# Six batches of Linformer attention inside a gated feed-forward kernel: from three mixed groups of TensorE work per batch to six single ones, with two Q buffers and the second batch's loads ahead of the loop

## The chip, the cores and the metric

One core of a Trainium2 chip. The metric is the device time of one execution in microseconds, lower being better. Engines are called PE (TensorE; PEld are its weight loads), DVE (VectorE), ACT (ScalarE), POOL (GpSimd) and SP (SyncE). POOL and SP issue the DMAs here.

## The reference

Eight batches (B = 8), eight heads, 1024 rows, head width 64. K and V are first projected along the rows to 64 by E and F, so that the scores of a head are 1024 x 64. A gated feed-forward layer follows.

```
k_proj = einsum('ks,bhsd->bhkd', E, k)
v_proj = einsum('ks,bhsd->bhkd', F, v)
scores = q @ k_proj^T / 8 ;  attn = softmax(scores)
x      = attn @ v_proj, heads side by side        # (8192, 512)
out    = (sigmoid(x @ w_gate) * (x @ w_val)) @ w_out   # 512 -> 1536 -> 512
```

Inputs and output are float32; the kernel's matmuls take bfloat16.

## The kernel before, in words

**A planner and five queues.** The program is a list of operations written in the order of the source. `add` (line 38) notes which tiles and PSUM banks an operation reads and writes; `emit` then gives each engine its own operations in that order, with a semaphore wait for each dependence on another engine. So the source order is the order of every queue, and nothing is reordered later. `mm`, `act`, `dve`, `pool` and `load` (lines 213 to 239) are the helpers that add to PE, ACT, DVE, POOL and POOL's DMA queue; all matmuls have line 221, all ACT instructions line 225, all loads line 239.

**PSUM.** Eight banks of 128 x 512 float32. Rings hand them out in turn: `ffn` has four (pF), `att` four (pA); the first batch uses `whole`, an order over both that is written out by hand.

**Feed-forward part.** A batch is two blocks of 512 rows. `mstep(blk, m)` (line 953) is one of 12 steps of a block: four matmuls for the gate (G), four for the value (V), each into an `ffn` bank; then `gate` (line 985): tanh on ACT from the G bank into `sig`, and on DVE `(sig + 1) * V` into `hT`. `oproj(blk, tt)` (line 1005) is an output projection: 12 matmuls, a scaling on DVE into `ost`, a DMA from SP. There are four per block, and they run during the next block.

**Slots.** For each batch b the loop at line 1095 makes a list `todo` of these pieces; the pieces are called slots here. For b >= 1 there are 32: with m for a step and o for a projection, slots 0 to 15 are m0 m1 m2 o0 m3 m4 m5 o1 m6 m7 m8 o2 m9 m10 m11 o3, and slots 16 to 31 the same for the second block. `put(i, fn)` hangs attention work of batch b+1 behind slot i. The iteration of batch b thus does the attention of batch b+1.

**Attention of a batch.** Its pieces: `kv`, 16 matmuls that project K and V into the halves of one bank; `keep_kd`, an ACT copy to `kpd` and a transposing DMA from SP into `kpD`; `keep_vd`, two ACT copies to `vpD`; `sc_one`, four score matmuls of 64 x 64 tiles for one pair of heads, and `exp_one`, two exponentials on ACT into `eT`; `den`, eight matmuls that sum `eT`; `rec(c)`, a reciprocal on DVE for a quarter of the columns; `gather`, four SP DMAs that bring the reciprocals into rows; `spread`, eight POOL broadcasts into `rb`; `xo_one`, four output matmuls for one pair of heads; `mul`, two DVE multiplications of the outputs with `rb` into `xT`, the input of the feed-forward part.

For batches 2 to 7 (iterations 1 to 6) the pieces stand in three groups on PE. `scores`: the scores of three of the four pairs, 12 matmuls, using two `ffn` and four `att` banks. `mixed`: the scores of the last pair and the outputs of two pairs, 12 matmuls. `outputs`: the outputs of the other two pairs, K and V of the batch after, and the sums, 32 matmuls. Outputs go from PSUM to SBUF on ACT (`keep_x`, into `xu`), and the multiplications read `xu`. The reciprocals hang on four slots, 12 to 15 or 17 to 20. In iteration 1 `kv2` at slot 3 projects K and V of batch 2.

Batch 0 and batch 1 are apart. Batch 0 runs in two halves (`half_unit`), the first before the loop, the second at slots 4 to 9 of iteration 0. Batch 1 (iteration 0) runs as single pieces: `k_alone`, `turn_k`, `sc(0)`, `sc(1)`, `den`, the reciprocals, `v_alone`, `split`, `bc`, `xo(0)`, `xo(1)`; there the multiplications read PSUM.

**Loads.** POOL's queue starts with batch 0 and the weights. `second_loads` (line 1076) follows slot 5 of iteration 0: Q, K and V of batch 1, Q's transposes on SP (`transpose_q`, four DMAs into `qT`), `wO`, a library for POOL. There is one Q buffer `Qb` and one `qT`; K and V turn through three `KV` buffers. `load_next` issues K, V and Q of a later batch.

Of the kernel before, what the change touches and what calls it, by code (L numbers as in the profile page):

```python
# [6 lines left out]
AF = mybir.ActivationFunctionType  # L7
ALU = mybir.AluOpType
# [4 lines left out]
P = 128  # L13
# [105 lines left out]
def bass_linformer_attn__then__ffn_glu_sigmoid_kernel(  # L119
# [18 lines left out]
    with contextlib.ExitStack() as es:  # L138
# [21 lines left out]
        Qb = sbuf("Qb", [P, H, S // P * DH], BF16)  # L160
# [5 lines left out]
        qT = sbuf("qT", [P, H, 512], BF16)  # L166
# [6 lines left out]
        xu = sbuf("xu", [P, 8, 512], FP32)  # L173
# [67 lines left out]
        def turned():  # L241
            return [("qT", r) for r in range(NR)]

        def load_k(b):
            n = 2 * b % 3
            load(
                KV[n][:, :, :],
                k[b].rearrange("h (p t) d -> p h (t d)", t=NT),
                [("KV", n, 0), ("KV", n, 1)],
                f"KV{n}",  # L250
                r=turned() if b >= 2 else (),
            )
# [19 lines left out]
        def load_q(b):  # L272
            load(
                Qb[:, :, :],
                q[b].rearrange("h (p t) d -> p h (t d)", t=NT),
                [("Q", hf, R) for hf in range(2) for R in range(2)],
                "Q",
            )

        def load_q_half(b, hf, R):  # L280
            cc, hh = slice(256 * hf, 256 * hf + 256), slice(4 * R, 4 * R + 4)
            load(
                Qb[:, hh, cc],
                q[b].rearrange("h (p t) d -> p h (t d)", t=NT)[:, hh, cc],
                [("Q", hf, R)],
                f"Q{hf}{R}",
            )
# [235 lines left out]
        def half_unit(hf, ring):  # L523

            s = 0
            qv = qT[:, :, :].rearrange("p (R x) c -> p R x c", R=2)

            def qt(R, engines):
                for rr, eng in enumerate(engines):
                    bk = ring.next()  # L530
                    ob = bank[bk][:, :].bitcast(BF16)
                    for x in range(2):
                        for t in range(2):
# [4 lines left out]
                                Qb[:, 4 * R + 2 * rr + x, (2 * hf + t) * P : (2 * hf + t + 1) * P],  # L538
                                ident[:, :],
                                [("Q", hf, R), "ident"],  # L540
# [4 lines left out]
                    ws = [("qT", hf, R, rr)]  # L545
# [5 lines left out]
            def sc(R):  # L551
                bks = [ring.next(), ring.next()]
                for rr in range(2):
                    for c in range(2):
                        h = 4 * R + 2 * rr + c
                        for g in range(2):
# [5 lines left out]
                                qT[gg, h, 256 * hf : 256 * hf + 256],  # L562
                                [("kpD", R), ("qT", hf, R, rr)],
# [94 lines left out]
        def transpose_q():  # L658
            for r in range(NR):
                add(  # L660
                    "SP",
                    lambda e, r=r: e.dma_start_transpose(
                        qT[:, 2 * r : 2 * r + 2, :].rearrange("p h (t c) -> p (h t) c", c=P),
                        Qb[:, 2 * r : 2 * r + 2, :].rearrange("p h c -> p (h c)"),
                    ),
                    r=[("Q", hf, r // 2) for hf in range(2)],
                    w=[("qT", r)] + [("qT", hf, r // 2, r % 2) for hf in range(2)],
                    dma=f"qT{r}",
                )

        def kv(b, bk):
            for t in range(NT):
                for w in range(2):
                    n = (2 * b + w) % 3
                    src = KV[n][:, :, :].rearrange("p h (t d) -> p t h d", t=NT)
                    mm(
                        bk,
                        bank[bk][64 * w : 64 * w + 64, :],
                        EFT[:, t, 64 * w : 64 * w + 64],
                        src[:, t, :, :],  # L680
                        [("KV", n, 0), ("KV", n, 1), ("EFT", t // 4)],
                        start=(t == 0),
                        stop=(t == NT - 1),
                        tp=(0, 64 * w),
                    )

        def keep_kd(bk):
            act(
                kpd[:, :, :, :],
                bank[bk][0:64, :]  # L690
                .rearrange("p (h d) -> p h d", h=H)
                .unsqueeze(2)
                .to_broadcast([64, H, 2, DH]),
                [],
                ["kpd"],
                b=bk,
            )
            add(
                "SP",
                lambda e: e.dma_start_transpose(  # L700
                    kpD[:, :, :],
                    kpd[:, :, :, :].rearrange("p h g d -> p (h g d)"),
                ),
                r=["kpd"],
                w=[("kpD", 0), ("kpD", 1)],
                dma="kpD",
            )

        def keep_vd(bk):
            for g in range(2):  # L710
                act(
                    vpD[64 * g : 64 * g + 64, :, :].rearrange("p h d -> p (h d)"),
                    bank[bk][64:128, :],
                    [],
                    [("vpD", h, g, R) for h in range(2) for R in range(2)],
                    b=bk,
                )

        def attention(b):
            s = b % 2  # L720
            den_bank = []

# [10 lines left out]
            def sc_one(r, bks):  # L733
                for c in range(2):
                    h = 2 * r + c
                    for g in range(2):
                        gg, oo = slice(64 * g, 64 * g + 64), 64 * (g ^ c)
                        mm(
                            bks[g],
                            bank[bks[g]][oo : oo + 64, :],  # L740
                            kpD[gg, h, :],
                            qT[gg, h, :],
                            [("kpD", r // 2), ("qT", r)],
                            tp=(64 * g, oo),
                        )

            def exp_one(r, bks):
                for g in range(2):
                    act(
                        eT[:, 2 * r + g, :],  # L750
                        bank[bks[g]][:, :],
                        [],
                        [("eT", 2 * r + g)],
                        b=bks[g],
                        func=AF.Exp,
                        scale=SCALE,
                    )

            def sc(r2):
                for r in (2 * r2, 2 * r2 + 1):  # L760
                    bks = [att.next(), att.next()]
                    sc_one(r, bks)
                    exp_one(r, bks)

            def den():
# [14 lines left out]
                den_bank.append(bk)  # L780

            def rec(c):
                cc, bk = slice(c * P, (c + 1) * P), den_bank[0]
# [54 lines left out]
            def xo_one(r, bks):  # L838
                for g in range(2):
                    n = 2 * r + g  # L840
                    for c in range(2):
                        kk = slice(64 * (g ^ c), 64 * (g ^ c) + 64)
                        mm(
                            bks[g],
                            bank[bks[g]][64 * c : 64 * c + 64, :],
                            vpD[kk, 2 * r + c, :],
                            eT[kk, n, :],
                            VPD(r // 2) + [("eT", n)],
                            tp=(64 * (g ^ c), 64 * c),
                        )  # L850

            def keep_x(r, bks):
                for g in range(2):
                    n = 2 * r + g
                    act(xu[:, n, :], bank[bks[g]][:, :], [], [("xu", n)], b=bks[g])

            def mul(r, bks=None):
                for g in range(2):
                    n = 2 * r + g
                    x = xu[:, n, :] if bks is None else bank[bks[g]][:, :]  # L860
                    dve(
                        lambda e, r=r, g=g, n=n, x=x: e.tensor_tensor(  # L862
                            xT[s][:, r, :, 256 * g : 256 * g + 256],
                            x.rearrange("p (f c) -> p f c", f=2),
                            rb[:, n, :].rearrange("p (f c) -> p f c", f=2),
                            ALU.mult,
                        ),
                        [("rb", n)] + ([("xu", n)] if bks is None else []),
                        [("xT", s, r, 0, g), ("xT", s, r, 1, g)],
                        b=None if bks is None else bks[g],  # L870
                    )

            def xo(r2):
                for r in (2 * r2, 2 * r2 + 1):
                    bks = [att.next(), att.next()]
                    xo_one(r, bks)
                    mul(r, bks)

            if b == 1:
# [5 lines left out]
                    lambda: (den(), rec(0)),  # L885
                    lambda: rec(1),
                    lambda: rec(2),
                    v_alone,
                    lambda: rec(3),
# [6 lines left out]

            held = {}

            def two(ring):
                return [ring.next(), ring.next()]  # L900

            def scores():
                f, a0, a1 = two(ffn), two(att), two(att)
                for r, bks in ((2, f), (0, a0), (1, a1)):
                    sc_one(r, bks)
                exp_one(2, f)
                exp_one(0, a0)
                held["sc"] = a1

# [284 lines left out]
```

## Time and profile before

| | |
|---|---|
| median of 3 runs (564.53 to 564.6) | 564.6 us |
| the profiled execution | 564.6 us |
| its span, first to last instruction | 562.8 us |
| granted TensorE clock | 1.000 |
| matmuls of the feed-forward part (wG, wV; wO) | 768 and 768; 780, of 3032 in all |
| mean of a 128 x 512 matmul, overlapping the next | 379 ns |
| tanh of a gate on ACT, x192 | 602 ns |
| gate's multiplication on DVE, x192 | 685 ns |
| multiplication xT<-xu,rb, x48; xT<-pA,rb, x8 | 856 ns; 680 ns |
| reciprocal of a quarter, x28 | 951 ns |

Busy shares are over the whole span. Matmuls overlap, so PE's price of a piece is read from starts, not from durations: the distance from the start of one matmul to the start of the next is its pitch. In the views below, "pF<-xT,wG" is a matmul into an `ffn` bank from `xT` and `wG`, "x4" the number merged in one line, and the two first columns are start and length in microseconds.

### The profile page before, as it was taken

The page shows a single profiled execution, that of the slowest core. Times are in us where ns is not written, and L with a number is a line of the kernel's source. Part 1 is how long each engine was busy: PE and PEld are TensorE (multiplying, and loading weights), DVE is VectorE, ACT ScalarE, POOL GpSimd, SP SyncE. Part 2 cuts the span into 40 slices and gives each one's busy share as a digit, 9 for nine tenths or more (in the row PEclk, how much of TensorE's full clock was granted, in tenths as well). Part 3 has the DMA queues.
Part 4 walks back from the last instruction along what each step waited for, and adds up shares of the span by engine and source line. Part 5 has one row for each costly group of instructions (what it writes and reads, how often), then busy time and mean ns, then how long its engine had stood idle before and what let it go on. Part 6 is the DMA issues. An engine that isn't in the chain of part 4 may idle for free.

```text
span 562.8 us, 7706 instructions
## 1 busy us (share of the span) xinstructions
PE 551.9 (98%) x3032; PEld 248.8 (44%) x3032; DVE 258.5 (46%) x397; ACT 200.8 (36%) x362; POOL 113.0 (20%) x148
## 2 busy tenths in 40 slices
PE   5899999999999999999999999999999999999998
PEld 4444434444444444444444444444444444444444
DVE  4544463325733564335643447335553357433332
ACT  2654633444244422534226422354224432222220
POOL 9210200102800190003600064000800026000000
PEclk9999999999999999999999999999999999999999
DMA  9999999953493259314591057901511101110012
GB/s 163 199 194 189 143 218 191 171 116 63 95 210 76 48 102 201 73 38 87 107 210 40 20 123 113 187 20 47 97 37 39 37 23 39 37 38 24 33 37 94
DMA packets 76564, 56.01 MB, mean 100 GB/s; under 512 B 34704, under 2 KB 68240, under 8 KB 76528
## 3 DMA queue, kind: packets, MB, share of 16 engines
q0 software_dynamic: 33984, 29.89, 34.6%
q1 hardware_dynamic: 42544, 25.63, 17.7%
q8 instruction: 24, 0.39, 0.3%
q14 instruction: 12, 0.10, 0.1%
HBM read 60.29 MB, written 16.78 MB: 137 GB/s over the span
## 4 chain that ended last, share of the span: by engine, by line
PE 96%; DMA 2%; DVE 1%; POOL 0%; issue 0%; ACT 0%; POOLq 0%
PE pF L221 90%; PE pA L221 6%; DMA Qb<-in_q_dram 2%; DVE xT L645 1%; POOL KV L239 0%; DVE hT L992 0%; DVE rden L593 0%; ACT qT L225 0%; POOL quad L313 0%; DVE rhl L596 0%; DVE ost L1023 0%; DVE rhi L594 0%; POOLq L1179 0%
## 5 line engine op out<-in xcount | busy, mean ns | idle before, releaser
L225 ACT ACTIVATE sig<-pF 128x512 f32<-128x512 f32 x192 | 115.5, 602 | 296.3 <-PE pF L221 290.6
L992 DVE SCALAR_TENSOR_TENSOR hT<-sig,pF 128x512 bf16<-128x512 f32 x192 | 131.4, 685 | 167.5 <-PE pF L221 129.0
L221 PE MATMUL pF<-xT,wG 128*128 128x512 bf16 x768 | 198.0, 379 | 1.2 <-DVE xT L645 1.2
L221 PE MATMUL pF<-xT,wV 128*128 128x512 bf16 x768 | 197.8, 379 | 0.3 <-DVE hT L992 0.3
L221 PE MATMUL pF<-wO,hT 128*128 128x512 bf16 (+1 forms) x780 | 175.7, 376 | 0.0
L831 POOL PARTITION_BROADCAST rb<-rrow x96 | 77.0, 862 | 286.3 <-DMA rrow<-rden 281.1
L221 PEld LDWEIGHTS pF<-wO,hT 128*128 128x128 bf16 x780 | 75.2, 98 | 91.4 <-issue 3.3
L221 PEld LDWEIGHTS pF<-xT,wV 128*128 128x128 bf16 x768 | 75.0, 98 | 91.1 <-DVE hT L992 0.8
L221 PEld LDWEIGHTS pF<-xT,wG 128*128 128x128 bf16 x768 | 72.9, 98 | 94.1 <-issue 8.7
L1023 DVE TENSOR_SCALAR ost<-pF 128x512 f32<-128x512 f32 (+1 forms) x65 | 44.4, 683 | 110.4 <-PE pF L221 110.4
L862 DVE TENSOR_TENSOR xT<-xu,rb 128x512 bf16<-128x512 f32 x48 | 39.2, 856 | 0.0
L785 DVE RECIPROCAL rden<-pA 128x128 f32<-128x128 f32 x28 | 26.6, 951 | 12.3 <-PE pA L221 12.3
L225 ACT ACTIVATE eT<-pA 128x512 bf16<-128x512 f32 x39 | 21.3, 626 | 1.6 <-PE pA L221 1.6
L225 ACT ACTIVATE eT<-pF 128x512 bf16<-128x512 f32 x25 | 13.6, 595 | 22.6 <-PE pF L221 22.4
L225 ACT ACTIVATE xu<-pA 128x512 f32<-128x512 f32 x36 | 19.1, 617 | 0.0
L221 PE MATMUL pA<-KV,EFT 128*64 128x512 bf16 (+2 forms) x168 | 16.0, 332 | 0.3
L239 POOL DMA_DIRECT2D KV<-in_k_dram x9 | 8.0, 885 | 34.5 <-PE pF L221 34.4
L239 POOL DMA_DIRECT2D Qb<-in_q_dram x11 | 9.4, 866 | 16.5 <-PE pF L221 16.5
L221 PEld LDWEIGHTS pA<-KV,EFT 128*64 128x64 bf16 x168 | 8.3, 115 | 7.8 <-issue 3.3
L225 ACT ACTIVATE vpD<-pA 64x512 bf16<-64x512 f32 (+2 forms) x22 | 10.2, 466 | 2.4 <-PE pA L221 1.9
L221 PE MATMUL pA<-eT,vpD 64*64 64x512 bf16 (+1 forms) x116 | 8.8, 355 | 0.0
L225 ACT ACTIVATE rb<-pA 128x512 f32<-128x512 f32 x14 | 7.4, 601 | 2.1 <-PE pA L221 2.1
(72 smaller groups left out, 122.3 us busy)
## 6 DMA issues: line engine op xcount, KB each, us to landing
out_dram<-ost SPq DMA_DIRECT2D x63, 256.0 KB, 2.0
Qb<-in_q_dram POOLq DMA_DIRECT2D x7, 1024.0 KB, 19.8
KV<-in_k_dram POOLq DMA_DIRECT2D x7, 1024.0 KB, 9.9
KV<-in_v_dram POOLq DMA_DIRECT2D x7, 1024.0 KB, 14.9
wO<-in_moe_w_out_dram POOLq DMA_DIRECT2D x1, 1536.0 KB, 12.2
wG<-in_moe_w_gate_dram POOLq DMA_DIRECT2D x5, 256.0 KB, 18.7
wV<-in_moe_w_val_dram POOLq DMA_DIRECT2D x5, 256.0 KB, 19.1
KV<-in_k_dram POOLq DMA_DIRECT2D x2, 512.0 KB, 8.9
```

What stands on the lines that cost most here:

```text
L221: return add("PE", lambda e: e.matmul(o, lhsT, rhs, **kw), r=r, x=[("bank", b)])
L225: return add("ACT", lambda e: e.activation(o, i, func, scale=scale), r=r, w=w, x=x)
L239: add("POOL", lambda e: e.dma_start(o, i), r=r, w=w, dma=sem)
L645: lambda e, g=g, o=o: e.tensor_tensor(o, bank[bks[g]][:, :].rearrange("p (r c) -> p r c", r=2), rb[:, 2 * R + g, :].rearrange("p (r c) -> ...
L785: lambda e: e.reciprocal(rden[:, cc], bank[bk][:, cc]),
L831: lambda e, n=n, i=2 * rnd + c, j=j, parts=parts: e.partition_broadcast(rb[0:parts, n, :], rrow[32 * j : 32 * j + 1, i, :], channels=parts),
L862: lambda e, r=r, g=g, n=n, x=x: e.tensor_tensor(xT[s][:, r, :, 256 * g : 256 * g + 256], x.rearrange("p (f c) -> p f c", f=2), rb[:, n, :] ...
L992: lambda e: e.scalar_tensor_tensor(hT[blk % 2][:, m, :], sg[:, :], 1.0, bank[pv][:, :], ALU.add, ALU.mult,),
L1023: lambda e, pb=pb, c0=c0, c1=c1: e.tensor_scalar(o[:, c0:c1], bank[pb][:, 0 : c1 - c0], 0.5, None, op0=ALU.mult),
```

## The change

Batches 2 to 7 no longer run in three mixed groups but as six single pieces per batch, all of the batch itself: `kv` at slot 3 (with its ACT copies), `turn_kd` at 6, `sc(0)` at 10, `sc(1)` at 13, `den` with its four reciprocals and then `gather` at 16, `spread` at 20 and 23, `xo(0)` at 26, `xo(1)` at 29. Each score or output piece is two pairs of heads, 8 matmuls. They use the `att` banks alone. `xu` and its copies go; the multiplications read PSUM. `Qb` and `qT` get a second buffer, picked by the batch's parity, and all names of their tiles get that index. `load_next` has the order K, Q, V. What was `second_loads` stands ahead of the loop. Batches 0 and 1 keep their pieces and slots.

```diff
-        Qb = sbuf("Qb", [P, H, S // P * DH], BF16)
+        Qb = [sbuf(f"Qb{i}", [P, H, S // P * DH], BF16) for i in range(2)]
-        qT = sbuf("qT", [P, H, 512], BF16)
+        qT = [sbuf(f"qT{i}", [P, H, 512], BF16) for i in range(2)]
-        xu = sbuf("xu", [P, 8, 512], FP32)
...
         def load_k(b):
-                r=turned() if b >= 2 else (),
+                r=turned(b - 1) if b >= 2 else (),
...
+            def turn_kd():
+                add("SP", lambda e: e.dma_start_transpose(kpD[:, :, :], ...),
+                    r=["kpd"], w=[("kpD", 0), ("kpD", 1)], dma="kpD")
...
             def den():
...
-                den_bank.append(bk)
+                if b == 1:
+                    den_bank.append(bk)
+                else:
+                    for c in range(4):
+                        rec(c, bk)
...
             def xo(r2):
                 for r in (2 * r2, 2 * r2 + 1):
                     bks = [att.next(), att.next()]
-                    xo_one(r, bks)
-                    mul(r, bks)
+                    for g in range(2):
...
+                            mm(bks[g], ..., VPD(r // 2) + [("eT", n)], tp=(64 * (g ^ c), 64 * c))
...
+                        dve(lambda e, r=r, g=g, n=n, bk=bks[g]: e.tensor_tensor(
+                                xT[s][:, r, :, 256 * g : 256 * g + 256],
+                                bank[bk][:, :].rearrange("p (f c) -> p f c", f=2),
+                                rb[:, n, :].rearrange("p (f c) -> p f c", f=2),
+                                ALU.mult), ...)
...
             return [
-                scores,
-                lambda: exp_one(1, held["sc"]),
-                mixed,
-                lambda: keep_x(1, held["x"]),
-                outputs,
-                lambda: (keep_x(3, held["x"]), rec(1)),
-                lambda: (rec(2), keep_kd(held["kv"]) if b + 1 < B else None),
-                lambda: (rec(3), gather(), keep_vd(held["kv"]) if b + 1 < B else None),
-                lambda: (spread(0), spread(1)),
-                lambda: mul(0),
-                lambda: mul(1),
-                lambda: mul(2),
-                lambda: mul(3),
+                kv,
+                turn_kd,
+                lambda: sc(0),
+                lambda: sc(1),
+                den,
+                gather,
+                lambda: spread(0),
+                lambda: spread(1),
+                lambda: xo(0),
+                lambda: xo(1),
             ]
...
-        def second_loads():
-            load_q(1)
-            load_k(1)
-            load_v(1)
-            transpose_q()
-            load(wO[:, :, :], ..., r=turned())
-            ...
+        load_q(1)
+        load_k(1)
+        load_v(1)
+        transpose_q(1)
+        load(wO[:, :, :], ..., r=turned(1))
...
-                put(5, second_loads)
...
-            elif b == 1:
-                put(3, kv2)
-                spots = (8, 9, 11, 12, 17, 18, 19, 20, 20, 25, 27, 28, 30)
             else:
-                spots = (3, 4, 6, 7, 12, 13, 14, 15, 15, 21, 23, 25, 27)
+                spots = (3, 6, 10, 13, 16, 16, 20, 23, 26, 29)
...
             def load_next(n):
                 load_k(n)
+                load_q(n)
                 load_v(n)
-                load_q(n)
...
-                put(24, transpose_q)
-            elif b + 2 < B:
-                put(4 if b == 1 else 1, lambda b=b: load_next(b + 2))
-                put(20 if b == 1 else 16, transpose_q)
+                put(24, lambda: transpose_q(2))
+            else:
+                if b + 2 < B:
+                    put(4, lambda b=b: load_next(b + 2))
+                    put(20, lambda b=b: transpose_q(b + 2))
```

## The prediction

> **What bounds the kernel now.** I read the page first, then who waited for whom on PE, then PE's own order of time around the attention groups, then single instructions on the other engines and the landings of the loads. The page's first part and its chain of waits:
>
> ```profile
> PE 551.9 (98%) x3032; PEld 248.8 (44%) x3032; DVE 258.5 (46%) x397; ACT 200.8 (36%) x362; POOL 113.0 (20%) x148
> ...
> PE 96%; DMA 2%; DVE 1%; POOL 0%; issue 0%; ACT 0%; POOLq 0%
> ```
>
> PE is 96% of the chain. The waits view, PE's lines:
>
> ```profile
> PE pA L221 <- DMA EF<-in_F_dram: 5.4, 1, 5.4
> PE pF L221 <- DVE xT L645: 1.2, 3, 0.8
> PE pA L221 <- DMA Qb<-in_q_dram: 0.5, 1, 0.5
> PE pF L221 <- DVE rhl L596: 0.4, 1, 0.4
> PE pF L221 <- DVE hT L992: 0.3, 1, 0.3
> ```
>
> All of these lie before 49 us (E, F and the first batch). From there to the end PE waits for nothing, so the later part costs what PE needs to push its instructions through. The stage view, cut at one batch of steady state (columns: stretch and length, then busy time and instructions of PE, weight loads, DVE, ACT and POOL, then granted clock, DMA share, GB/s):
>
> ```profile
> 229.69:296.65 66.96, 66.96 (x350) 29.55 (x344) 31.25 (x45) 24.36 (x43) 15.26 (x19) 1.00 0.50 97
> ```
>
> The next three batches take 66.96 us each too, all at a granted clock of 1.00. 288 of the matmuls are the feed-forward part's. PE's order of time gives their pitch: eight start between 163.09 and 164.82, 0.216 us each, so 62.2 us; the other 4.8 us are attention. **The question is only what attention costs PE in the new grouping.** The price of a group is the start of the feed-forward matmul after it, less the start of the run before it, less 0.216 for each matmul of that run. The old groups (scores; scores with outputs; outputs with K/V and sums):
>
> ```profile
> 161.57 0.81 PE L221 MATMUL pF<-wO,hT 128*128 128x512 bf16 x3
> 162.31 0.41 PE L221 MATMUL pF<-qT,kpD 64*64 64x512 bf16 x4
> 162.55 0.60 PE L221 MATMUL pA<-qT,kpD 64*64 64x512 bf16 x8
> 163.09 1.04 PE L221 MATMUL pF<-xT,wG 128*128 128x512 bf16 x4
> ...
> 180.38 1.03 PE L221 MATMUL pF<-xT,wV 128*128 128x512 bf16 x4
> 181.34 0.41 PE L221 MATMUL pF<-eT,vpD 64*64 64x512 bf16 x4
> 181.57 0.39 PE L221 MATMUL pA<-eT,vpD 64*64 64x512 bf16 x4
> 181.89 1.92 PE L221 MATMUL pA<-KV,EFT 128*64 128x512 bf16 x16
> 183.74 0.61 PE L221 MATMUL pA<-eT,dsel 128*32 128x512 bf16 x8
> 184.29 1.04 PE L221 MATMUL pF<-xT,wG 128*128 128x512 bf16 x4
> ```
>
> 163.09 - 161.57 - 3 x 0.216 = 0.87 us for twelve; the mixed group at 168.37 also has twelve and also costs 0.87; 184.29 - 180.38 - 4 x 0.216 = 3.05 us for the third. One batch: 0.87 + 0.87 + 3.05 = 4.79. The second batch still runs the old small groups, which are the ones that the change brings back:
>
> ```profile
> 56.88 1.03 PE L221 MATMUL pF<-xT,wV 128*128 128x512 bf16 x4
> 57.84 0.63 PE L221 MATMUL pA<-qT,kpD 64*64 64x512 bf16 x8
> 58.39 1.04 PE L221 MATMUL pF<-xT,wG 128*128 128x512 bf16 x4
> ```
>
> 58.39 - 56.88 - 0.864 = 0.65 for eight score matmuls (0.67 for the next eight). By the same subtraction the eight matmuls of the sums at 62.63 cost 0.70, the eight outputs at 79.11 and at 82.37 cost 0.65 each, and the sixteen of K and V alone at 93.39 cost 1.94. Twelve cost 0.87 and eight 0.65, so four packed ones take one pitch, 0.216, and some 0.22 of each group is going in and coming out.
>
> **Part by part.**
>
> *Regrouping.* Six batches, iterations 1 to 6. Before: iteration 1 has K/V alone and the three groups, 1.94 + 4.79 = 6.73; iterations 2 to 5 have 4.79 each; iteration 6 has no K/V, 0.87 + 0.87 + 1.20 = 2.94 (its last group at 449.22 costs 1.20). Sum 28.8. After: 1.94 + 0.65 + 0.67 + 0.70 + 0.65 + 0.65 = 5.26, times six = 31.6. **+2.8 us.** Same matmuls; what is added is three more goings in and out per batch, less the two changes of kind inside the third group, which cost 3.05 - (0.43 + 1.73 + 0.43) - 0.22 = 0.24 together.
>
> *Copies into xu gone.* 48 ACT copies (25.6 us busy) go, and the 48 multiplications read PSUM: 0.68 us as in the second batch in place of a mean 0.856. Neither stands on the chain: worth 0. Its counterpart is that a multiplication now holds the bank of its output. xo(0) and xo(1) come three slots apart, some 6 us, and four multiplications took 2.47, so the banks are free.
>
> *Four reciprocals in a row, after slot 16.* Counted from the end of slot 16: the gate of slot 16 runs at 0.27 to 0.9, the sums end on PE at 0.7, the reciprocals run from 1.0 to 4.9 (0.95 each). Queued behind them on DVE is the gate of slot 17, ready at 2.7, now 4.9 to 5.5, then that of slot 18, to 6.2. PE needs the V bank of slot 17 again for slot 20; slot 19 is an output projection of 2.59 us on another bank, so that is at 0.70 + 2 x 1.73 + 2.59 = 6.7. Cover 1.2 us: cost 0. Without slot 19's projection it would be 1.4 us a batch, 8 in all.
>
> *Gather and spread.* The SP copies follow the last reciprocal; in the old trace POOL began 2.3 us after it and took 13.6 us for 16 broadcasts. That gives 7.2 to 14 for the first eight and 21 for the rest; xo(0) comes at 19.7 and xo(1) at 26.4. Cost 0, with 5 us in hand.
>
> *Last multiplications.* xo(1) after slot 29: the multiplications end some 3.4 us later; the next batch's first matmul comes after slots 30 and 31, 0.65 + 1.73 + 2.59 = 5.0. Cost 0; 1.6 us in hand.
>
> *K turned in the same batch.* kpd takes 1.0 on ACT, its DMA landed after 2.7 to 3.0 us, in iteration 1 with three loads issued just behind it. Slots 4 to 10 last 13.0. Only the result DMA of slot 3 stands ahead of it on SP. Cost 0, 8 us in hand; without those slots it would be some 4 us a batch.
>
> *Two Q and qT buffers, loads as k, q, v.* In iterations from 1 on POOL issues the K and Q loads earlier and V's behind K/V of slot 3; nothing but the next broadcasts is queued behind. The tight place is the third batch: its loads landed at 77.4 (k), 83.2 (v) and 90.1 (q), and PE wants K and V at 93.4. Now v is last, so 90.1, and Q's four transposes start at 83.5 on SP beside it. The second batch's case: its v took 6.7 us beside transposes against 5.3 for k before it, +1.4. So 91.5 against 93.4: cost 0, with 2 us in hand.
>
> *Second loads ahead of the loop.* POOL issues them at 17.7 instead of 34.4. They stand behind the weights in one queue; the last weight landed at 39.0 and q at 44.3, k at 49.6, at 5.3 us apiece, so that queue was never empty and landings stay. The first output projection reads wO at 73.4 and it landed at 72.3: 1 us in hand, unchanged. New is that the three issues (0.88 each, 17.7 to 20.4) lie beside DVE's chain of the first sums, which PE waits for. Twelve equal instructions that build dsel beside POOL's load issues took 234 ns at the shortest and 570 at the longest, and the long ones end with a load issue (at 5.22 and 5.96). Two casts (17.94 and 19.57) may be caught so: 0 to 2 x 0.34 = 0.7; a multiplication with both inputs in SBUF at 210.2, beside a load issue, was not slowed. I take **+0.3**, the middle, since each cast stands near an edge of an issue.
>
> [...]
>
> **Sum.** The profiled execution: span 562.8, and 564.6 with what lies around it, equal to the median of the three runs. 564.6 + 2.8 + 0.3 = **567.7 us**.
>
> **Rivals.** About 0.2%, 1.1 us, can be told from no change.
>
> (1) *Faster*: the 0.22 of a group is not a price of every group but belongs to the second batch's crowded stage. The six groups need 1.94 - 0.21 + 0.43 x 5 = 3.9 us of pure pitch; they cost less than 4.79 as soon as a group's overhead is under 0.15. At 0.10 it is 4.5 a batch, 1.8 us less over six: 562.8. Against it: 0.22 is the same at 57.8 and 162.3, and operands were long ready in both. 6%.
>
> (2) *No visible change*, the overhead near that point: 564.6 and at most 1.1 off. 5%.
>
> (3) *V of the third batch late*: needs the transposes to delay it by over 3.3 us instead of 1.4. Up to 2 us once: 568.7. 12%.
>
> (4) *DVE's run of reciprocals becomes the bound*: needs DVE to be 1.2 us later than in my count, for example by ACT's tanh lagging. Each half microsecond beyond costs 6 x 0.5: 570.7. 9%.
>
> (5) *wO late*: 1 us in hand at the start; 1 us once: 568.7. 6%.
>
> **How the numbers follow.** My forecast has 62%, its own range 566.9 to 568.5 (startup 0 to 0.7, prices of groups within 0.03 each, 6 x 6 x 0.02 = 0.7). With (3), (5) and the near half of (4) the range is 566.6 to 569.8. Faster 0.06; within 0.2%, 0.06 (rival 2 and the edge of the forecast); slower 0.88.
>
> **What would show it.** Right: stages of 67.43 us per batch; six groups per batch at 0.65 to 0.70 and 1.94; no PE waits after 50 us; feed-forward start at about 21.9 instead of 21.6. Wrong: a PE wait on hT or on a KV load, a group price that differs from the second batch's, or a start later than 22.4.

## The result, and the profile after

The changed kernel takes 567.5 us (median of four runs, 567.1 to 568.4) against 564.6 for the kernel before (four runs, 564.3 to 564.6). The ratio is 1.0055, 95% interval 1.0037 to 1.0072: slower by 0.55%, and 567.7 was forecast. The execution that was profiled is the longest of the four, 568.35 with a span of 566.5; the other spans are 566.1, 565.2 and 565.2.

The page's first part and its chain of waits, of the kernel after:

```profile
PE 556.0 (98%) x3032; PEld 247.5 (44%) x3032; DVE 248.8 (44%) x397; ACT 177.6 (31%) x314; POOL 107.4 (19%) x148
...
PE 95%; DMA 2%; DVE 1%; POOL 1%; ACT 0%; issue 0%; POOLq 0%
```

ACT lost 23.2 us of work and DVE 9.7, as the xu copies and the slower multiplications went, and the kernel became longer all the same: 95% of the chain is still PE, and where the copies and multiplications went neither engine stands on it. PE has the same 3032 matmuls and is busy 4.1 us longer. What it waited for (us in total, times, longest):

```profile
PE pA L220 <- DVE dsel L398: 5.6, 1, 5.6
PE pF L220 <- DVE xT L645: 0.9, 2, 0.7
PE pF L220 <- DVE rhl L596: 0.4, 1, 0.4
PE pA L220 <- DMA Qb<-in_q_dram: 0.4, 1, 0.4
PE pF L220 <- DVE hT L940: 0.3, 1, 0.3
```

The first is the wait for E and F again, put down here to another releaser. All lie before 51 us, as before, so no new wait came. The stage view, cut at one batch (stretch and length, then busy time of PE, weight loads, DVE, ACT, POOL, clock, DMA share, GB/s):

```profile
229.44:296.86 67.42, 67.42 (x346) 29.24 (x346) 29.80 (x44) 20.45 (x35) 14.32 (x19) 1.00 0.49 96
```

67.42 us where it was 66.96 and 67.43 was forecast. PE's order of time shows the groups (start, length, x the number merged):

```profile
161.29 0.81 PE L220 MATMUL pF<-wO,hT 128*128 128x512 bf16 x3
162.03 1.92 PE L220 MATMUL pA<-KV,EFT 128*64 128x512 bf16 x16
163.88 1.04 PE L220 MATMUL pF<-xT,wG 128*128 128x512 bf16 x4
...
175.98 1.03 PE L220 MATMUL pF<-xT,wV 128*128 128x512 bf16 x4
176.93 0.63 PE L220 MATMUL pA<-qT,kpD 64*64 64x512 bf16 x8
177.49 2.76 PE L220 MATMUL pF<-wO,hT 128*128 128x512 bf16 x12
```

163.88 - 161.29 - 3 x 0.216 = 1.94 for K and V; 177.49 - 175.98 - 4 x 0.216 = 0.65 for eight scores. The second scores and both outputs cost 0.65 too, the sums 0.64: 5.18 a batch, 31.1 for six, against 28.8.

**Where the 3.7 us between the two profiled spans (562.8 and 566.5) lie.** The chain that ended last has these pieces of PE (start, length): K and V of the third batch and the last stretch, first before, then after:

```profile
93.46 1.85 PE pA L221 x16
450.39 109.79 PE pF L221 x520
```
```profile
94.69 1.85 PE pA L220 x16
486.97 76.99 PE pF L220 x368
```

From K and V of the third batch to the end of the last matmul it was 560.18 - 93.46 = 466.72; it is 563.96 - 94.69 = 469.27. That is 2.55 us, the regrouping. The distance does not vary: it is the same to 0.01 us in all five profiles with the six single groups (after, a1, a2, a3, b1 below) and in both with the old groups (before and a4). The other 1.2 came earlier, and the stage view of the start says how (same columns as the stage view above):

```profile
18.30:21.70 3.40, 2.37 (x48) 1.56 (x49) 3.06 (x6) 2.72 (x9) 2.23 (x3) 1.00 1.41 193
21.71:25.12 3.41, 3.41 (x15) 0.95 (x15) 1.29 (x2) 1.28 (x3) 0.00 (x0) 0.50 1.45 196
```

For 3.41 us the granted clock was 0.50 (the last columns are clock, DMA share, GB/s). The feed-forward matmuls of that stretch start 0.43 us apart instead of 0.216. The kernel before had 1.00 there in its profile. Whether that belongs to the change was the first question.

### The profile page after: what moved, and what is told of

Same layout as the page of the kernel before. It is cut to its first block, busy times and chain, and to the rows that moved or that the text cites. A ratio compares the mean times of both kernels' runs of the same rounds, so it can differ in the third digit from the quotient of the medians.

```text
span 566.5 us, 7713 instructions
## 1 busy us (share of the span) xinstructions
PE 556.0 (98%) x3032; PEld 247.5 (44%) x3032; DVE 248.8 (44%) x397; ACT 177.6 (31%) x314; POOL 107.4 (19%) x148
## 4 chain that ended last, share of the span: by engine, by line
PE 95%; DMA 2%; DVE 1%; POOL 1%; ACT 0%; issue 0%; POOLq 0%
PE pF L220 89%; PE pA L220 7%; DMA KV<-in_v_dram 2%; DVE xT L645 1%; POOL KV L238 0%; POOL Qb L238 0%; DVE hT L940 0%; ACT rb L224 0%; ACT vpD L224 0%; POOL quad L313 0%; DVE ost L971 0%; POOLq L1116 0%
## 5 line engine op out<-in xcount | busy, mean ns | idle before, releaser
L829 POOL PARTITION_BROADCAST rb<-rrow x96 | 70.9, 799 | 217.1 <-DMA rrow<-rden 211.9
L224 ACT ACTIVATE eT<-pA 128x512 bf16<-128x512 f32 x63 | 32.7, 605 | 8.5 <-PE pA L220 8.5
L854 DVE TENSOR_TENSOR xT<-pA,rb 128x512 bf16<-128x512 f32 x56 | 34.6, 680 | 0.0
L783 DVE RECIPROCAL rden<-pA 128x128 f32<-128x128 f32 x28 | 24.1, 915 | 0.0
L238 POOL DMA_DIRECT2D KV<-in_v_dram x9 | 7.8, 873 | 82.4 <-PE pF L220 82.4
L224 ACT ACTIVATE kpd<-pA 64x1024 bf16<-64x1024 f32 x6 | 6.1, 1017 | 28.3 <-PE pA L220 28.3
L220 PE MATMUL pA<-eT,vpD 64*64 64x512 bf16 (+1 forms) x140 | 10.6, 374 | 0.0
L220 PE MATMUL pA<-qT,kpD 64*64 64x512 bf16 (+1 forms) x140 | 10.6, 367 | 0.0
```

The lines of the kernel that those rows point to most:

```text
L220: return add("PE", lambda e: e.matmul(o, lhsT, rhs, **kw), r=r, x=[("bank", b)])
L224: return add("ACT", lambda e: e.activation(o, i, func, scale=scale), r=r, w=w, x=x)
L238: add("POOL", lambda e: e.dma_start(o, i), r=r, w=w, dma=sem)
L783: lambda e: e.reciprocal(rden[:, cc], bank[bk][:, cc]),
L829: lambda e, n=n, i=2 * rnd + c, j=j, parts=parts: e.partition_broadcast(rb[0:parts, n, :], rrow[32 * j : 32 * j + 1, i, :], channels=parts),
L854: lambda e, r=r, g=g, n=n, bk=bks[g]: e.tensor_tensor(xT[s][:, r, :, 256 * g : 256 * g + 256], bank[bk][:, :].rearrange("p (f c) -> p f c" ...
```

## The experiments

Beside a1 to a4 the kernel before ran 24 times: 563.7 to 566.4, median 564.87. So its runs vary by 2.7 us, more than the first four had shown. Beside b1 to b4 it ran 8 times: 564.4 to 565.3, median 564.74.

Every run also has its mean granted clock. One window of 3.41 us at 0.50 makes a mean of 0.997 of such a span, which is what the profiled execution above has. In 7 of the 24 runs of the kernel before it is 0.997 too (565.4 to 566.4 us). So a stretch of that kind comes without the change, which answers the question; where in the run it lies there, the mean does not say. It is 0.997 in 1 of 9 runs of a1, 2 of 9 of a2, 3 of 12 of a4 and none of 7 of a3.

**a1_again: the changed kernel, unedited.**

> The changed kernel once more, for the spread of its runs: four runs so far had spans of 565.2, 565.2, 566.1 and 566.5, the last one with a stretch of 3.4 us at a granted clock of 0.50 near 22 us. Theory A (a clock window that falls on the thin stretch at 18 to 22 us by chance): most runs at 566.9 to 567.2, some 1 us longer, and the same long ones are seen now and then in the kernel before too. Theory B (the early loads of batch 1 make the start longer): the long ones are seen here only. Both: median 567.0 to 567.6.

Nine runs: 566.13 to 568.31, median 567.09; ratio 1.0035 (1.0022 to 1.0048). Four lie between 567.0 and 567.1, two at 566.13. The shortest run is 2.42 over the shortest of the kernel before, the median 2.22. Among the runs at a mean clock of 1.000 alone (8 here, 17 of the kernel before) the medians are 567.05 and 564.65, 2.40 apart. The profile has no stretch at 0.50 while the program runs, but another delay. DVE's order of time, this run:

```profile
17.04 0.95 DVE L593 RECIPROCAL rden<-pF 64x128 f32<-64x128 f32 x1 [0.86 <-PE pF L220]
18.02 0.78 DVE L594 CAST rhi<-rden 64x128 bf16<-64x128 f32 x1
18.84 0.34 DVE L596 SCALAR_TENSOR_TENSOR rhl<-rhi,rows,rden 64x128 bf16<-64x128 bf16 x1
19.21 0.96 DVE L593 RECIPROCAL rden<-pA 64x128 f32<-64x128 f32 x1
20.21 0.34 DVE L594 CAST rhi<-rden 64x128 bf16<-64x128 f32 x1
```

and POOL's in the same run:

```profile
17.74 1.02 POOL L238 DMA_DIRECT2D Qb<-in_q_dram  x1
18.61 1.01 POOL L238 DMA_DIRECT2D KV<-in_k_dram  x1
19.48 1.02 POOL L238 DMA_DIRECT2D KV<-in_v_dram  x1
```

The first cast took 0.78 us and ended at 18.80, just behind the end of Q's issue (18.76). The second took 0.34 and ended at 20.55, just behind V's (20.50). In the first profile of the changed kernel, where DVE was 0.08 earlier, the same cast was free:

```profile
17.94 0.22 DVE L594 CAST rhi<-rden 64x128 bf16<-64x128 f32 x1
```

There Q's issue ran from 17.76 to 18.78 and the cast began 0.18 us into it; in a1 it began 0.28 us into it. The first feed-forward matmul starts at 22.62 in a1 and at 21.64 there. Of these 0.98 us the two casts are 0.68 (0.56 and 0.12) and the later start of DVE 0.08; the rest lies between the last multiplication and that matmul.

**a2_late: the loads of batch 1 written behind slot 5 again.**

```diff
-        load_q(1)
-        load_k(1)
-        load_v(1)
+        def second_loads():
+            load_q(1)
+            load_k(1)
+            load_v(1)
...
                 put(5, lambda: (sc2(0), sc2(1)))
+                put(5, second_loads)
```

> The changed kernel with the loads of batch 1 back behind slot 5, all else as changed. Theory A: the same mixture as the changed kernel, median 567.0 to 567.6. Theory B: no long runs, every one at 564.6 + 2.4 = 567.0 within 0.2. Either way the six single groups, 6 x (1.94 + 4 x 0.65 + 0.64) = 31.1 against 28.8, remain: not under 566.7.

567.04 median of nine (566.99 to 569.58). It tells nothing of late loads, since they were not late: POOL issued Q at 17.73, as in a1. With two Q buffers nothing is left for the load to wait for, and POOL works through its queue far ahead of PE; the place in the source only sets the order in each queue. It is the changed kernel once more. Its profile shows the free case: first cast at 17.86, 0.22 us long, first feed-forward matmul at 21.77, span 565.2. Its two longest runs (568.9, 569.6) have a mean clock of 0.997; neither was profiled.

**a3_fill: 14 more filler matmuls behind bc(1).**

```diff
         bc(1)
+        busy(14)
         load_q(1)
```

> The changed kernel with 14 more filler matmuls where PE waits for the first xT, 20.8 to 21.6 us (0.75 us of work in a wait of 0.9). Theory A: PE is busy in every clock window, no long runs, all at 567.0 within 0.2. Theory B (something other than an idle PE, such as loads that land later): the long runs stay.

Seven runs, 566.92 to 568.24, median 567.22. The long runs stay, at a mean clock of 1.000, so theory A alone does not hold. In its profile (span 566.1) the first cast began at 18.11 and took 0.69, first feed-forward matmul at 22.62, no clock at 0.50. None of the seven runs had the slow window; beside 7 of 24 in the kernel before that is too few to say that the fillers prevent it.

**a4_before_early: the kernel before with two Q buffers and early loads.**

```diff
-        Qb = sbuf("Qb", [P, H, S // P * DH], BF16)
+        Qb = [sbuf(f"Qb{i}", [P, H, S // P * DH], BF16) for i in range(2)]
...
+        load_q(1)
+        load_k(1)
+        load_v(1)
+
         def second_loads():
-            load_q(1)
-            load_k(1)
-            load_v(1)
```

> The kernel before with a second Q buffer and the three loads of batch 1 issued ahead of the loop; the three mixed groups and one qT stay. Theory A: 564.6, with now and then a run 1 us longer. Theory B: the long runs appear here, 564.6 in some and 565.5 to 565.9 in others. Either way far under 567.0, if the regrouping is what costs 2.4.

Twelve runs, 563.60 to 567.98, median 565.33; ratio 1.0008, interval 0.9992 to 1.0023. So the early loads alone are +0.46 us in the median, which the interval doesn't tell from none, and not the 2.4. Its profile has both delays: the first cast at 18.08 took 0.72, and the clock was 0.50 in this stretch:

```profile
21.17:24.58 3.41, 3.08 (x35) 1.54 (x33) 1.46 (x3) 2.17 (x6) 0.00 (x0) 0.50 1.45 196
```

So the window at 0.50 does not need the new grouping. Of its nine runs at a mean clock of 1.000 three lie at 564.45 to 564.58 and five at 565.32 to 565.41. That is what two values of the start 0.85 us apart would give, but only one run of the kernel was profiled.

**b1_wait: Q of batch 1 waits for the turns of batch 0's Q.** This stands on top of the edit of a2, so that the three loads are written behind slot 5 and Q has something to wait for there.

```diff
-                [("Q", s, hf, R) for hf in range(2) for R in range(2)],
+                [("Q", i, hf, R) for i in ((0, 1) if b == 1 else (s,)) for hf in range(2) for R in range(2)],
```

> The changed kernel with the load of batch 1's Q made to wait for the second half of batch 0's Q turns, as in the kernel before (in a2 it was moved in the source, but POOL still issued it at 17.7). Theory B (cast shut out by POOL's load issue): the first cast takes 0.22 us in every profile, never 0.7 to 0.8, first feed-forward matmul at 21.6 to 21.8; the runs that are 0.85 longer go, and runs with a clock window at 0.50 may remain as in the kernel before. Theory A (only the clock window): the same mixture as a1. Regrouping stays: 2.4 over the kernel before.

Five runs: 566.88, 567.11, 567.37, 567.56, 568.77; ratio 1.0051 (1.0037 to 1.0065). First feed-forward matmul at 21.61, as theory B has it. But the first cast took 0.46 and not the 0.22 that was expected: the first half of K had landed at 8.35 instead of some 9.4, DVE was earlier, and the cast of 17.46 met the issue of the last weight chunk (17.00 to 17.88). So even late loads leave an issue to be caught by, and a long run remained (568.77, at a mean clock of 1.000). Theory B has a real mechanism, but it isn't the only source of the spread.

**b2_split: ten groups per batch.** Each score and output piece is cut into its two pairs of heads, a slot apart:

```diff
-                lambda: sc(0),
-                lambda: sc(1),
+                lambda: sc(0, [0]),
+                lambda: sc(0, [1]),
+                lambda: sc(0, [2]),
+                lambda: sc(0, [3]),
...
-                spots = (3, 6, 10, 13, 16, 16, 20, 23, 26, 29)
+                spots = (3, 6, 10, 11, 13, 14, 16, 16, 20, 23, 25, 26, 28, 29)
```

> The changed kernel with each of the four score and output pieces cut in two, a slot apart: ten groups per batch instead of six, the same matmuls. Theory G (a group costs 0.22 us for going in and out, whatever is in it): four matmuls alone cost 0.216 + 0.22 = 0.44, so 4 x 6 x 0.22 = 5.3 us more, a batch 67.42 + 0.87 = 68.29, 572.4 in all. Rival (the cost is in the kinds of matmul, not in how often they are entered): 567.1.

573.45 median of four (573.44 to 574.52), 6.4 over a1. PE's order of time, and one batch in the stage view:

```profile
108.10 1.03 PE L220 MATMUL pF<-xT,wV 128*128 128x512 bf16 x4
109.06 0.41 PE L220 MATMUL pA<-qT,kpD 64*64 64x512 bf16 x4
109.40 2.76 PE L220 MATMUL pF<-wO,hT 128*128 128x512 bf16 x12
```
```profile
230.81:299.13 68.32, 67.84 (x338) 29.19 (x344) 29.91 (x44) 20.55 (x35) 14.29 (x19) 1.00 0.48 95
```

109.40 - 108.10 - 0.864 = 0.436 for four matmuls, and a batch takes 68.3 us. Both are as theory G has them: four more entries, 4 x 0.22 = 0.88, take a batch from 67.42 to 68.3. The rival is out. Of the 6.4, 5.6 lie behind K and V of the third batch (474.9 to the end of the last matmul, against 469.3), where the groups are. The other 0.85 lie ahead: its profile has the held cast (0.59, first feed-forward matmul at 22.62, against 21.77 in a2).

**b3_rec8: the reciprocals twice.**

```diff
                     for c in range(4):
                         rec(c, bk)
+                    for c in range(4):
+                        cc = slice(c * P, (c + 1) * P)
+                        dve(lambda e, cc=cc: e.reciprocal(rden2[:, cc], bank[bk][:, cc]),
+                            [], [("rden2", c)], b=bk)
```

> The changed kernel with the four reciprocals behind the sums done twice, the second time into a tile that nothing reads: 3.4 us more on DVE in slots 17 to 20. Theory C (the run of reciprocals is hidden with under 2 us to spare): the gate of slot 17 comes 1.6 us after PE wants its bank, so 1.6 x 6 = 9 to 10 us more, 576 to 577, and PE waits for hT. Rival (DVE is far off the path): 567.1.

575.83 (575.83 to 576.70), 8.7 over a1, a little under the 9 to 10 expected. DVE and PE around slots 16 to 20 in this run:

```profile
260.19 3.39 DVE L792 RECIPROCAL rden<-pA 128x128 f32<-128x128 f32 x4
263.50 3.33 DVE L783 RECIPROCAL rden<-pA 128x128 f32<-128x128 f32 x4
266.75 1.22 DVE L949 SCALAR_TENSOR_TENSOR hT<-sig,pF 128x512 bf16<-128x512 f32 x2
```
```profile
PE pF L221 <- DVE hT L949: 8.5, 7, 1.5
```

The gates of slots 17 and 18 stand behind the second four, and PE waits for the first of them, 8.5 us in all over six batches (and once at the start). The stage is hidden, but with less than one more run of reciprocals to spare.

**b4_sc7: the scores three slots earlier.**

```diff
-                spots = (3, 6, 10, 13, 16, 16, 20, 23, 26, 29)
+                spots = (3, 6, 7, 10, 16, 16, 20, 23, 26, 29)
```

> The changed kernel with the scores behind slots 7 and 10 instead of 10 and 13. Theory K (kpD's transposing DMA shares with the loads in flight and lands 7 to 9 us late, as its trace has it, with 1.9 to 4.6 us in hand at slot 10): stalls of 2.6, 0.9, 0.6, 3.3, 2.6 and 0 us in iterations 1 to 6, 10 us in all, 577, PE waiting for the DMA of kpD. Rival, the forecast's row (kpD lands 2.7 to 3.0 us after its issue, 8 us in hand): 567.1.

581.73 (580.86 to 582.64), 14.6 over a1. The waits view, and PE and the stages around the first of these stalls:

```profile
PE pA L220 <- DMA kpD<-kpd: 10.2, 5, 3.4
```
```profile
106.27 1.07 PE L220 MATMUL pA<-qT,kpD 64*64 64x512 bf16 x8 [3.05 <-DMA kpD<-kpd]
107.27 1.89 PE L220 MATMUL pF<-xT,wG 128*128 128x512 bf16 x4
```
```profile
102.35:105.76 3.41, 0.88 (x5) 0.20 (x2) 0.69 (x1) 0.00 (x0) 0.00 (x0) 1.00 1.22 182
105.77:109.18 3.41, 2.91 (x13) 0.93 (x14) 0.00 (x0) 2.07 (x4) 0.00 (x0) 0.50 1.19 239
```

Ten microseconds of stalls, five of them, as theory K has it. The other 4 us were not foreseen: from 105.77, inside the stall of 103.2 to 106.3, the clock was 0.50 for 3.41 us (the four G matmuls at 107.27 take 1.69 us to the next start, not 0.86), and again for 6.83 us from 314.0, inside the longest stall (3.39 us, to 314.88) and behind it. If PE gets half as much done there, it loses (109.18 - 106.27) / 2 + (320.83 - 314.88) / 2 = 4.4 us by this estimate, which is what was left to explain. Behind the other three stalls (0.9, 0.5 and 2.3 us) no window at 0.50 came.

## Why the prediction was right

**The close hit is partly luck.** 567.7 was forecast and 567.5 is the median of four runs, of which two ran at 567.1. The other two were longer: one by the stretch at a clock of 0.50, which the forecast did not have, and one at 567.88 with the span of 566.1 that the profiles with a held cast have in a1 and a3. Nine more runs gave 567.09. That lies within the range, 0.6 under the forecast.

**Regrouping, +2.8: the mechanism holds, the size was 2.4 to 2.55.** The distance from the third batch's K and V to the end grew by 2.55 in the profiles, the shortest runs differ by 2.42, the medians of 9 and 24 runs by 2.22 (2.40 at a mean clock of 1.000). b2 shows that the price is per entry: cutting groups without another change costs 0.22 each. Two prices that I took from the second batch were too high: its second scores at 0.67 and its sums at 0.70. There they come one slot behind the pieces that they wait for: the last exponentials of ACT end at 62.85, and the sums' matmuls begin at 62.63 and hold. Three slots apart they cost 0.65 and 0.64. By the prices of the new trace the sum is 31.1 - 28.8 = 2.3, half a microsecond (six times 0.08) under mine, and the measured 2.55 lies between the two. So the stage of 67.43 us was hit in part by luck: the groups of a batch grew by 0.39 (5.18 from 4.79), the batch by 0.46, and I have no row for the rest.

**Early loads, +0.3 (0 to 0.7): the mechanism is there, and its size is two-valued.** In a1, a3 and a4 the first cast began 0.28 to 0.38 us into POOL's issue of Q and ended at 18.80, 0.04 to 0.05 behind that issue's end (0.69 to 0.78 long); b2's ended at 18.80 too (0.59). In the first profile and in a2 it began 0.13 to 0.18 us into that issue and was not held (0.22). In those four the first feed-forward matmul starts at 22.6 to 22.9, in these two at 21.6 to 21.8. One of my signs of being wrong, a start later than 22.4, so came true in those four executions. The first cast lost up to 0.56, more than the 0.34 that I had read from the building of dsel; the second lost 0.12 in the same four (0.34 against 0.22). Averaged over executions the early loads are worth +0.46 in a4, not told from none.

**What I left out: the clock.** The forecast had no clock below 1.00. In the profiled execution a window at 0.50 cost 1.2 us: the first feed-forward matmul starts at 21.64 as in the profile before, K and V of the third batch 1.23 us later. In a4's it cost some 0.7 (K and V of the third batch at 94.87, in a1 and a3 at 94.15). It hits some executions and not others, of the kernel before too (a mean clock of 0.997 in 7 of its 24 runs). The stretches at 0.50 were 3.41 us long, and once 6.83, in b4. What decides stays open. Ahead of the one in the changed kernel's first profile PE was busy for 2.37 of 3.40 us (18.30 to 21.70). In a1, with a mean clock of 1.000, it was busy for 2.35 us from 17.14 to 20.55 and for 2.27 from 20.55 to 23.96, so as little work in a stretch of that length was not followed by 0.50 there.

**Edits priced at nothing.** The reciprocals: cover 1.2 us by my count. The four took 3.39 us instead of 3.9, since a row of them overlaps (0.89 to 0.96 us each, started some 0.83 apart), and the first of the two gates behind them ended near 262.5 where PE wanted its bank at 264.4, so the cover was some 1.8; b3 confirms that a second run of 3.3 us overruns it, by about 1.4 us a batch. The last multiplications: DVE finished them at 287.4, in time. V of the third batch landed at 90.4 and was wanted at 94.6. wO landed at 72.7 and was wanted at 74.6. Rivals 3, 4 and 5 did not come.

**Where the working was wrong without cost: kpD.** The forecast has "8 us in hand" from a landing 2.7 to 3.0 us after the issue. This is how the landings of that DMA stand (us, shortest, median, longest of six), in the kernel before and in the changed one:

```profile
DMA to landing us min/median/max: 2.7/2.7/3.0
```
```profile
DMA to landing us min/median/max: 2.7/8.4/9.9
```

In the kernel before the DMA ran with no load beside it, or with loads issued after it; now V's load is issued just ahead of it in each iteration that has one, and it takes about three times as long (7.2 to 9.9 us in iterations 1 to 5, 2.7 in iteration 6, which has no load). In iteration 4 it landed at 309.89 for scores at 311.76. There were 1.9 us in hand, not 8, and b4 shows what lies beyond: 10 us of stalls. That no cost came is owed to the distance between the slots, not to the working.

**The faster rival** needed an entry under 0.15 us. It is 0.22 in every group measured, for four, eight and twelve matmuls.

**Open.** How often the held cast comes was not settled: there is one profile per kernel, and the spread of the runs of one kernel (0.9 to 4.4 us) is as wide as the effects. What brings a stretch at 0.50, and what the shortest runs (566.1 here, 563.6 to 563.7 in a4 and before) did otherwise, is open too. A kernel whose early loads start only after the second cast was not run. No version here beats the kernel before; its three mixed groups are the cheapest grouping tried.

## What to carry to other kernels

Where PE is the bound, price small packed matmuls by group, not by matmul: here 0.22 us for every excursion from the large matmuls and back, so gather them into few. Copies and multiplications taken off engines that wait anyway (33 us of ACT and DVE here) bought nothing. A landing time read from a quiet place in a trace did not hold here where the edit put a large load ahead of it (2.7 us became 7.2 to 9.9): look at what is in flight at the new place, and count the distance to the user again.

## What the runs showed that I had not expected

An extra Q buffer moved a load by 17 us without its line moving: the old place was enforced by the buffer, and in a2 writing the load later changed nothing.

Two of five stalls of PE, the two over 3 us, were paid for again afterwards: b4's 10.2 us of waits came with 4 us more, and the clock was 0.50 for 3.41 us once and for 6.83 us once.

One DVE cast of 0.22 us in the first profile took 0.78 in a1, where it began 0.08 us later and ended 0.04 us behind the end of POOL's issue of a load. The casts are on the chain of the first batch: where the first was held, the feed-forward part started 0.85 to 1 us later, of which 0.68 in a1 are the two casts.
